# A written order for the first eight attention blocks, and moves of splits, sums and loads behind it

## The chip, the cores and the metric

The kernel runs on one core of a Trainium2 chip. A core has five engines with an instruction queue each: TensorE (PE in the views) for matrix products, VectorE (DVE), ScalarE (ACT), GpSimd (POOL) and SyncE (SP), which here only issues DMA transfers. The metric is the time of one execution in device microseconds, as a median of several runs; the profile is of one execution more, whose span is given beside it. TensorE's clock has two levels, 1.2 and 2.4 GHz; the granted clock in the views is the mean share of the upper one.

## The reference

Windowed attention, then a mixture of four experts, then a second feed-forward layer, all in float32 (w_in, w_out and alpha are drawn in float64):

```python
B, H, S, D = 2, 8, 576, 64                  # window 64
scores = q @ k.T / sqrt(D);  mask = (0 <= rel) & (rel < 64)
attn = exp(where(mask, scores, -1e9) - max);  attn /= sum + 1e-9
x = (attn @ v)                              # -> (1152, 512)
p = probs / (probs.sum(-1) + 1e-9)
y = sum(p[:, e] * (relu(x @ w1[e]) @ w2[e]) for e in range(4))    # w1 512 x 1024
h = y @ w_in                                # 512 x 2048
out = (max(h, 0) + alpha * min(h, 0)) @ w_out
```

## The kernel before, in words

Every product outside attention is done in three passes with operands split into a high part (rounded to fp32r) and a low part (the rest): high by low, low by high, high by high. ACT makes the high part, DVE or POOL the low part. So each operand tile, of weights or of tokens, costs one copy and one subtraction, and each result of a first product costs a copy (the activation) and a subtraction for its own halves, which the second product reads. In names, the last letter h or l is the part: w1h, w1l, xah, xal, hch, hcl.

**Stages.** The hidden width is cut into pieces of 512: stages 0 to 7 are the experts (two pieces each), stages 8 to 11 the second layer. A stage has first products and second products. In stages 1 to 11 the first products are seven per token half and column pair (a Strassen-like scheme over sums of weight blocks and of token blocks; units `A(s, p, i)`, banks X, Z and W in the views), and the second products are nine tiles of 128 tokens (units `B(s, p, t)`, tiles o). Stage 0 is done in four chunks of tokens without that scheme, since the tokens come out of attention at the same time: units `LC(c, f)` are the first products (tiles h0_c_f), units `BC(c, t)` the second ones (tiles oc). The list `order` holds all units in the order in which TensorE does them.

**Attention.** There are 18 blocks j of 64 queries. A block is a sequence of steps, and the list `steps` sets their order: `S` (scores, TensorE) with the mask and row minimum on DVE (sm, st), `E` (exponentials, four ACT instructions, p), `N` (divisors on two small DVE instructions, then p times them on POOL), `PT` (transposes on TensorE and the copy ptr on ACT or DVE), `PV` (product with v, and its splits into xah/xal or xch/xcl), `W` (a split of a stage-0 weight piece, `split_w1`), `Q` (a load of q), `X` (a token sum and split for the scheme, tiles tr and xt). Before the first unit the program emits steps up to the chunk's last PV and four steps more; behind each LC and BC unit it emits some more, until all are out at END.

**Behind the units.** After the unit's own instructions the loop runs what `plan` has put there: `w_sums` (four sums of weight blocks on POOL, tile sr), `w_split` (wfh, wfl), `split_w2` (w2h, w2l), and for stage 8 `x_sum` and `x_split` of the new tokens. From chunk 3 on, low parts are emitted one unit later than their high parts (`late["wait"]`, `settle`). Then come as many steps of a background job as `pace` gives: `conv_steps` turns the float64 pieces of w_in and w_out into float32 (32 pieces, tiles wd and ct; a step on ACT, one on DVE, one on DVE with the next load, one on DVE and POOL with a store to DRAM later). Last come the loads of weights, which are placed behind the last use of the tile whose buffer they take. In stages 8 to 11 the activation has more steps: `activate` runs a DVE step (heads) and then a copy on ACT and a subtraction on POOL (tails, hh and hl), of which some may be held back.

All queues are in program order. So what an engine does next is set by where these lists put it, and an instruction that waits holds what stands behind it on its engine.

## Time and profile before

| | before |
|---|---|
| median of 3 runs | 633.32 us (632.99 to 634.52) |
| profiled execution | 634.3 us |
| its span | 632.5 us |
| TensorE busy | 612.8 us (97%) |
| DVE, ACT, POOL busy | 462.6, 315.7, 285.4 us |
| mean granted clock | 0.992 |

The span is what the profile shows from the first to the last instruction; 1.8 us of the profiled execution lie outside of it. Busy times add an engine's instructions; a matmul's end is modelled, so a starved TensorE can look busy. TensorE's share of 97% means that at most 20 us of the span are without a matmul, 5.58 of them ahead of the first one.

### The profile page before, as it was taken

The page shows a single profiled execution, that of the slowest core. Times are in us where ns is not written, and L with a number is a line of the kernel's source. Part 1 is how long each engine was busy: PE and PEld are TensorE (multiplying, and loading weights), DVE is VectorE, ACT ScalarE, POOL GpSimd, SP SyncE. Part 2 cuts the span into 40 slices and gives each one's busy share as a digit, 9 for nine tenths or more (in the row PEclk, how much of TensorE's full clock was granted, in tenths as well). Part 3 has the DMA queues.
Part 4 walks back from the last instruction along what each step waited for, and adds up shares of the span by engine and source line. Part 5 has one row for each costly group of instructions (what it writes and reads, how often), then busy time and mean ns, then how long its engine had stood idle before and what let it go on. Part 6 is the DMA issues. An engine that isn't in the chain of part 4 may idle for free.

```text
span 632.5 us, 10897 instructions
## 1 busy us (share of the span) xinstructions
PE 612.8 (97%) x4032; PEld 548.9 (87%) x4032; DVE 462.6 (73%) x933; ACT 315.7 (50%) x789; POOL 285.4 (45%) x301
## 2 busy tenths in 40 slices
PE   4899999999999999999999999999999999999998
PEld 3688789989989988989989988989788978988986
DVE  3766649778789788788789788757867789763642
ACT  5756526633724624624724624636766662751730
POOL 5645651143443466053443463614735676661440
PEclk8899989999999999999999999999999999999999
DMA  9842001415316225324316224012302124110012
GB/s 323 310 153 68 2 1 64 138 33 183 118 46 205 84 84 183 100 68 167 118 54 196 84 83 150 18 35 98 135 1 108 59 103 136 34 63 1 2 50 101
DMA packets 31653, 62.60 MB, mean 99 GB/s; under 512 B 2288, under 2 KB 11760, under 8 KB 30576
## 3 DMA queue, kind: packets, MB, share of 16 engines
q1 hardware_dynamic: 31600, 61.90, 29.0%
q8 instruction: 32, 0.52, 0.3%
q14 instruction: 21, 0.17, 0.1%
HBM read 51.14 MB, written 10.75 MB: 98 GB/s over the span
## 4 chain that ended last, share of the span: by engine, by line
PE 83%; DVE 5%; ACT 4%; DMA 2%; POOL 2%; issue 2%; SPq 0%; ACTq 0%; POOLq 0%; DVEq 0%
PE o L545 40%; PE X L431 19%; PE Z L431 9%; PE W L431 4%; PE oc L533 4%; PE h L500 3%; ACT p L327 1%; DMA ws<-in_moe_w_dram 1%; PE pv L357 1%; DMA wd<-in_moe_w_in_dram 1%; POOL hl L526 1%; PE s L309 1%; DVE w2l L212 1%; PE pt L340 1%; ACT w2h L219 1%
## 5 line engine op out<-in xcount | busy, mean ns | idle before, releaser
L545 PE MATMUL o<-w2h,hl 128*128 128x512 f32 (+1 forms) x400 | 155.7, 389 | 0.6 <-POOL hl L526 0.5
L545 PE MATMUL o<-w2l,hh 128*128 128x512 f32 (+1 forms) x400 | 155.6, 389 | 0.4 <-ACT hh L525 0.4
L545 PE MATMUL o<-w2h,hh 128*128 128x512 f32 (+1 forms) x400 | 154.9, 387 | 0.0
L292 POOL TENSOR_TENSOR ct<-ct 128x512 f32<-128x512 f32 x32 | 42.7, 1335 | 133.3 <-DVE ct L291 58.1
L545 PEld LDWEIGHTS o<-w2h,hl 128*128 128x128 f32 x400 | 75.1, 188 | 18.3 <-POOL hl L526 3.2
L545 PEld LDWEIGHTS o<-w2l,hh 128*128 128x128 f32 x400 | 75.2, 188 | 15.0 <-ACT hh L525 0.6
L545 PEld LDWEIGHTS o<-w2h,hh 128*128 128x128 f32 x400 | 75.2, 188 | 14.9
L564 DVE SCALAR_TENSOR_TENSOR acc<-o,pn,acc 128x512 f32<-128x512 f32 x63 | 47.1, 748 | 40.7 <-PE o L545 40.6
L187 POOL TENSOR_TENSOR sr<-ws 128x256 f32<-128x256 f32 x44 | 41.6, 944 | 58.9 <-DVE wfl L212 53.0
L212 DVE SCALAR_TENSOR_TENSOR w2l<-ws,w2h 128x512 fp32r<-128x512 f32 x48 | 43.8, 918 | 25.6 <-ACT w2h L219 25.2
L431 PE MATMUL X<-xth,wfl 128*128 128x256 f32 (+1 forms) x264 | 57.4, 298 | 2.8 <-DVE z L442 1.7
L431 PE MATMUL X<-xtl,wfh 128*128 128x256 f32 (+1 forms) x264 | 56.6, 296 | 0.0
L431 PE MATMUL X<-xth,wfh 128*128 128x256 f32 (+1 forms) x264 | 56.6, 296 | 0.0
L293 POOL TENSOR_TENSOR ct<-ct 128x512 f32<-128x512 f32 x32 | 48.3, 1508 | 2.5
L280 ACT ACTIVATE ct<-wd 128x512 f32<-128x512 f32 x32 | 21.3, 665 | 50.8 <-DVE ct L286 50.8
L219 ACT ACTIVATE wfh<-sr 128x1024 fp32r<-128x1024 f32 x22 | 23.1, 1056 | 45.8 <-POOL sr L187 45.8
L431 PEld LDWEIGHTS X<-xth,wfl 128*128 128x128 f32 x264 | 42.5, 190 | 3.8 <-DVE z L442 2.3
L431 PEld LDWEIGHTS X<-xth,wfh 128*128 128x128 f32 x264 | 42.7, 190 | 0.0
L431 PEld LDWEIGHTS X<-xtl,wfh 128*128 128x128 f32 x264 | 42.6, 190 | 0.0
L568 DVE TENSOR_TENSOR acc<-o,acc 128x512 f32<-128x512 f32 (+1 forms) x28 | 18.7, 668 | 29.7 <-PE o L545 29.7
L526 POOL TENSOR_TENSOR hl<-s,hh 128x256 fp32r<-128x256 f32 (+1 forms) x16 | 13.4, 860 | 56.7 <-ACT hh L525 56.7
L438 ACT ACTIVATE s<-X 128x256 f32<-128x256 f32 (+1 forms) x44 | 18.0, 411 | 40.1 <-PE X L431 40.0
(157 smaller groups left out, 1440.5 us busy)
## 6 DMA issues: line engine op xcount, KB each, us to landing
ws<-in_moe_w_dram SPq DMA_DIRECT2D x16, 1024.0 KB, 5.9
wd<-in_moe_w_in_dram SPq DMA_DIRECT2D x16, 512.0 KB, 3.8
cv<-ct SPq DMA_DIRECT2D x32, 256.0 KB, 3.0
wd<-in_moe_w_out_dram SPq DMA_DIRECT2D x16, 512.0 KB, 3.7
ws<-cv SPq DMA_DIRECT2D x8, 1024.0 KB, 5.2
v<-in_v_dram SPq DMA_DIRECT2D x16, 256.0 KB, 5.4
q<-in_q_dram SPq DMA_DIRECT2D x6, 384.0 KB, 6.7
out_dram<-acc SPq DMA_DIRECT2D x8, 256.0 KB, 2.0
```

The source lines that it names most:

```text
L187: e.tensor_tensor(out=t4[:, o], in0=x, in1=y, op=op)
L212: nc.vector.scalar_tensor_tensor(out=lv, in0=src, scalar=1.0, in1=hv.bitcast(F32), op0=ALU.mult, op1=ALU.subtract)
L219: nc.scalar.activation(out=hv, in_=src, func=AF.Copy)
L280: nc.scalar.activation(out=a, in_=top.bitcast(F32), func=AF.Abs, scale=LIFT)
L292: nc.gpsimd.tensor_tensor(out=y, in0=y, in1=e, op=ALU.mult)
L293: nc.gpsimd.tensor_tensor(out=y, in0=r, in1=y, op=ALU.add)
L431: nc.tensor.matmul(ps, lhsT=w[:, d, :], rhs=x[:, d, :], start=(first and m == 0), stop=(m == 5), skip_group_check=True)
L500: nc.tensor.matmul(ps, lhsT=w[:, d * P:(d + 1) * P], rhs=x[:, d, :], start=(m == 0), stop=(m == 3 * KD - 1))
L526: nc.gpsimd.tensor_tensor(out=hl, in0=g, in1=hh.bitcast(F32), op=ALU.subtract)
L533: nc.tensor.matmul(ps, lhsT=h_c[c, f][a][:, t * P:(t + 1) * P], rhs=w_t[2, 0, f][b], start=(n == 0), stop=(n == 3 * NF - 1))
L545: nc.tensor.matmul(ps, lhsT=h_t[s, p, f][a][:, t * P:(t + 1) * P], rhs=w_t[2, s, f][b][:, cols], start=(n == 0), stop=(n == 3 * NF - 1))
L564: nc.vector.scalar_tensor_tensor(out=at, in0=ps, scalar=sc, in1=at, op0=ALU.mult, op1=ALU.add)
```

## The change

The first 8 blocks' steps are written out by hand, with four blocks' exponentials one behind the other; the mask on DVE becomes a step `M` of its own. The splits of stage-0 weight pieces 2 and 3 move behind the first two LC units, the second ones' w2 splits by one unit; the even pieces' low parts go to DVE and the odd ones' to POOL, where it was the other way round. From block 8 on a loop goes on as before, with the X steps one block earlier and the last block's N ahead of a PT. Loads of w1 pieces from stage 2 on are placed no earlier than behind the fourth product of the stage before; some sums and splits of weights, the token sums of stage 8 and the steps of the conversion move to other units.

```diff
--- before.py
+++ after.py
@@ -226,7 +226,7 @@
         hv, lv = [x.rearrange("p (k m) -> p k m", k=KD) for x in w_tiles(1, 0, f)]
         src = ws_t[1, 0][:, :, f * P:(f + 1) * P]
         nc.scalar.activation(out=hv, in_=src, func=AF.Copy)
-        e = nc.vector if f % 2 else nc.gpsimd
+        e = nc.gpsimd if f % 2 else nc.vector
         e.tensor_tensor(out=lv, in0=src, in1=hv.bitcast(F32), op=ALU.subtract)
 
     def split_w2(s, f):
@@ -294,7 +294,7 @@
             done.append((conv[which, s][:, f, :], ct[:, 4 + n % 3]))
         store()
 
-    v_t, ws_t, wd_t, w_t, wf_t, h_t, p_t, pt_t = {}, {}, {}, {}, {}, {}, {}, {}
+    v_t, ws_t, wd_t, w_t, wf_t, h_t, m_t, p_t, pt_t = {}, {}, {}, {}, {}, {}, {}, {}, {}
 
     def att_S(j):
         g, jb = divmod(j, GB)
@@ -313,6 +313,10 @@
                     start=True, stop=True, skip_group_check=True,
                 )
 
+        m_t[j] = sv, m
+
+    def att_M(j):
+        sv, m = m_t.pop(j)
         sm = ab.tile([P, NP, P], F32, tag="sm", bufs=2, name=f"sm{j}")
         st = ab.tile([P, 4, NP], F32, tag="st", bufs=4, name=f"st{j}")
         pt = ab.tile([P, NP, P], F32, tag="p", bufs=4, name=f"p{j}")
@@ -340,7 +344,7 @@
             nc.tensor.transpose(ps[:, hp * P:(hp + 1) * P], pt[:, hp, :], ident)
         t = ab.tile([P, NP, P], F32, tag="ptr", bufs=2, name=f"ptr{j}")
         src = ps.rearrange("p (a k) -> p a k", a=NP)
-        if j % 2 and j >= NF:
+        if j in (0, 1) or j % 2 and j >= NF:
             nc.vector.tensor_copy(out=t, in_=src)
         else:
             nc.scalar.activation(out=t, in_=src, func=AF.Copy)
@@ -361,7 +365,7 @@
         c = max(c for c in range(NCH) if CHUNK[c] <= j * BLK)
         o = j * BLK - CHUNK[c]
         hi, lo = [x[:, :, o:o + BLK] for x in xc[c]]
-        if (j + 1) * BLK in CHUNK:
+        if j == 2 or (j + 1) * BLK in CHUNK:
             nc.scalar.activation(out=hi, in_=pv, func=AF.Copy)
             nc.vector.tensor_tensor(out=lo, in0=pv, in1=hi.bitcast(F32), op=ALU.subtract)
             nc.vector.tensor_copy(out=src, in_=pv)
@@ -458,7 +462,7 @@
             evict(s, p, 2 * u + 1, 0, ps, True)
             del sets[s, p, u]
         if s >= S1:
-            activate(1 if i > 2 else 0, int(i < 5) if s == S1 else (2, 0, 4)[min(i, 2)])
+            activate(1 if i > 2 else 0, 0 if s == S1 else (2, 0, 4)[min(i, 2)])
         else:
             low_parts(1)
 
@@ -601,37 +605,35 @@
         nc.sync.dma_start(out=alph, in_=alpha)
 
         NG = NBLK // GB
-        steps = []
-        for j in range(NBLK + 4):
+        steps = [(op, int(j)) for op, j in (x.split("_") for x in (
+            "S_0 M_0 E_0 S_1 M_1 E_1 N_0 S_2 M_2 E_2 N_1 S_3 M_3 E_3 Q_3 PT_0 N_2 PT_1 N_3 PV_0 W_0 PT_2 PV_1 W_1 "
+            "S_4 M_4 PT_3 PV_2 PV_3 S_5 E_4 M_5 N_4 E_5 S_6 M_6 N_5 Q_4 E_6 PT_4 S_7 M_7 N_6").split())]
+        for j in range(8, NBLK + 4):
             last = (j - 3) * BLK in CHUNK[1:]
-            pv = [("PV", j - 4)] if 0 <= j - 4 < NBLK else []
-
+            pv = [("PV", j - 4)] if j - 4 < NBLK else []
+            apart = j - 1 < 14
             if last:
                 steps += pv
-            apart = 6 <= j - 1 < 14
             if apart:
                 steps.append(("E", j - 1))
-            if 0 <= j - 3 < NBLK:
+            if j == NBLK:
+                steps.append(("N", j - 1))
+            if j - 3 < NBLK:
                 steps.append(("PT", j - 3))
-            if 3 < j <= NBLK and not apart:
+            if not apart and j < NBLK:
                 steps.append(("N", j - 1))
             if j < NBLK:
-                steps.append(("S", j))
-                if not 6 <= j < 14:
+                steps += [("S", j), ("M", j)]
+                if j >= 14:
                     steps.append(("E", j))
-            if 0 < j <= 3:
-                steps.append(("N", j - 1))
             if not last:
                 steps += pv
             if apart:
                 steps.append(("N", j - 1))
-            if 2 <= j < 2 + NF:
-                steps.append(("W", j - 2))
-            if j % GB == 0 and 3 <= j // GB + 2 < NG:
+            if j % GB == 0 and j // GB + 2 < NG:
                 steps.append(("Q", j // GB + 2))
-
-            if 13 <= j < 18:
-                steps.append(("X", j - 13))
+            if 12 <= j < 17:
+                steps.append(("X", j - 12))
         pos = [0]
 
         def att_step():
@@ -643,6 +645,8 @@
                     load_k(1, 0, S)
             elif op == "S":
                 att_S(j)
+            elif op == "M":
+                att_M(j)
             elif op == "E":
                 att_E(j)
             elif op == "N":
@@ -695,8 +699,10 @@
         def plan(unit, fn, tid, *args):
             work.setdefault(at[unit], []).append((fn, tid, args))
 
+        for f in range(2, NF):
+            plan(("LC", 0, f - 2), split_w1, None, f)
         for f in range(NF):
-            plan(("LC", 0, f), split_w2, (2, 0), 0, f)
+            plan(("LC", 0, min(f + 1, 3)), split_w2, (2, 0), 0, f)
         for s in range(1, NST):
             if s == 1:
                 lc, b = [[(k, NCH - 1, t) for t in range(3)] for k in ("LC", "BC")]
@@ -709,13 +715,15 @@
                 b = [("B", s - 1, x, t) for x in range(2) for t in range(NTT[x])]
                 if s == S1 + 1:
                     b = [("B", S1, 1, t) for t in (3, 3, 4, 4, 0, 1)]
-                plan(("A", s - 1, 1, 0 if s > S1 else 2), w_sums, (1, s), s, 0, nc.gpsimd)
-                plan(b[2], w_sums, (1, s), s, 1, nc.gpsimd)
-                for n, part in ((0, A11), (0, A22), (1, SA1)):
+                late_sums = s > S1 + 1
+                behind = 2 * (s > S1 + 1)
+                plan(b[1] if behind else ("A", s - 1, 1, 0 if s > S1 else 2), w_sums, (1, s), s, 0, nc.gpsimd)
+                for n, part in ((0, A11), (0, A22), (1 + behind, SA1)):
                     plan(b[n], w_split, (1, s), s, 0, part)
-                for n, part in ((2, A11), (3, A22), (4, SA1)):
+                plan(b[2 + behind], w_sums, (1, s), s, 1, nc.gpsimd)
+                for n, part in ((2, A11), (3, A22), (4 + behind, SA1)):
                     plan(b[n], w_split, (1, s), s, 1, part)
-            units = [(0, 1), (0, 2), (1, 0), (1, 1)]
+            units = [(0, 0), (0, 1), (1, 0), (1, 1)]
             if s in (1, S1):
                 units = [(int(s == 1), i) for i in (0, 0, 1, 1)]
             for f, (p, i) in enumerate(units):
@@ -729,9 +737,11 @@
                    (("B", S1 - 1, 1, 2), 0, (3, 5), (), first), (("B", S1 - 1, 1, 3), 0, (3, 5), (), second),
                    (("B", S1 - 1, 1, 4), 0, (4,), (), first), (("B", S1 - 1, 1, 4), 0, (4,), (), second)]
         for o in half[1]:
-            changes += [(("A", S1, 0, 2), 1, (), (1,), o), (("A", S1, 0, 3), 1, (), (2,), o),
-                        (("B", S1, 0, 2), 1, (0, 1), (), o), (("B", S1, 0, 3), 1, (2,), (3,), o),
-                        (("B", S1, 0, 0), 1, (3, 5), (4,), o), (("B", S1, 0, 1), 1, (4,), (), o)]
+            changes += [(("B", S1, 0, 2), 1, (0,), (1,), o), (("B", S1, 0, 3), 1, (1,), (), o),
+                        (("B", S1, 0, 0), 1, (2, 5), (3,), o), (("B", S1, 0, 1), 1, (3,), (), o),
+                        (("A", S1, 1, 0), 1, (4,), (), o)]
+        for unit, f in ((("B", S1, 0, 2), 2), (("B", S1, 0, 1), 4)):
+            changes += [(unit, 1, (), (f,), o) for o in half[1]]
         for unit, p, splits, sums, (o, w) in changes:
             for f in splits:
                 if f == 0:
@@ -764,24 +774,27 @@
                     uses.setdefault(tid, []).append(n)
         tids = sorted(uses, key=lambda x: uses[x][0])
         tids = [(1, 0)] + tids
-        uses[1, 0] = [-1]
+        uses[1, 0] = [at["LC", 0, 1]]
         loads = {}
         for n, tid in enumerate(tids):
             if n >= 2:
-                loads.setdefault(uses[tids[n - 2]][-1] + (tids[n - 2][1] > 0), []).append(tid)
+                free = uses[tids[n - 2]][-1] + (tids[n - 2][1] > 0)
+                if tid[0] == 1 and tid[1] > 1:
+                    free = max(free, at["A", tid[1] - 1, 0, 3])
+                loads.setdefault(free, []).append(tid)
 
         marks = [steps.index(("PV", CHUNK[c + 1] // BLK - 1)) + 1 for c in range(NCH)]
         per = [len(LC(c) + BC(c)) for c in range(NCH)]
-        while pos[0] < marks[0] + 4:
+        while pos[0] < marks[0] + 2:
             att_step()
         for tid in loads.get(-1, ()):
             load_w(tid)
         def pace(op, s=0, p=0, i=0):
             if op == "A":
-                return int(2 <= s < S1 and i < 2 + (s == S1 - 1) or S1 < s < NST - 1 and i in (1, 2))
-            if op != "B" or s in (S1 - 1, NST - 2, NST - 1) or (s, p) == (S1, 0):
+                return int(2 <= s < S1 and i < 2 or S1 < s < NST - 1 and i < 2)
+            if op != "B" or s in (S1 - 1, NST - 2, NST - 1) or (s, p) == (S1, 0) or s > S1 and (p, i) == (0, 0):
                 return 0
-            return 1
+            return 1 + (s == 1 and p == 0 and i % 2)
 
         pend = []
         for i, unit in enumerate(order):
@@ -813,7 +826,7 @@
                 l2_unit(*unit[1:])
                 if unit[1] == S1 - 1:
                     pend.append((i + 2, unit[2], unit[3]))
-            if i == 0:
+            if i == 2:
                 p_prep()
             while pend and pend[0][0] <= i:
                 x2_unit(*pend.pop(0)[1:])
```

How this moves instructions on three engines. ACT, from the first weight copy on (block 3's exponentials are p3; w1h_0_f are the copies of stage 0's weight pieces). Before:

```order
L327 ACTIVATE p2_219,st2_218<-sm2_217,st2_218 128x128 x4
L228 ACTIVATE w1h_0_0_231<-ws1_0_147 128x512
L346 ACTIVATE ptr0_240<-pt0_235 128x512
L327 ACTIVATE p3_254,st3_253<-sm3_252,st3_253 128x128 x4
L228 ACTIVATE w1h_0_1_266<-ws1_0_147 128x512
L346 ACTIVATE ptr1_277<-pt1_272 128x512
L327 ACTIVATE p4_294,st4_293<-sm4_292,st4_293 128x128 x4
L228 ACTIVATE w1h_0_2_317<-ws1_0_147 128x512
L346 ACTIVATE ptr2_326<-pt2_321 128x512
L327 ACTIVATE p5_343,st5_342<-sm5_341,st5_342 128x128 x4
L228 ACTIVATE w1h_0_3_366<-ws1_0_147 128x512
L346 ACTIVATE ptr3_375<-pt3_370 128x512
```

After:

```order
L331 ACTIVATE p2_219,st2_218<-sm2_217,st2_218 128x128 x4
L331 ACTIVATE p3_243,st3_242<-sm3_241,st3_242 128x128 x4
L228 ACTIVATE w1h_0_0_288<-ws1_0_147 128x512
L350 ACTIVATE ptr2_297<-pt2_292 128x512
L228 ACTIVATE w1h_0_1_313<-ws1_0_147 128x512
L350 ACTIVATE ptr3_339<-pt3_334 128x512
L369 ACTIVATE xah0_81<-pv2_341 128x4x64
L369 ACTIVATE xah0_81<-pv3_355 128x4x64
L331 ACTIVATE p4_329,st4_328<-sm4_327,st4_328 128x128 x4
L515 ACTIVATE hch0_0_397<-h0_0_0_384 128x256
L228 ACTIVATE w1h_0_2_401<-ws1_0_147 128x512
L331 ACTIVATE p5_407,st5_406<-sm5_405,st5_406 128x128 x4
```

p3 and the weight copies changed places, ptr0 and ptr1 left ACT, the second part of xah came to it, and the copies of weight pieces 2 and 3 stand behind the first two products' copies hch.

DVE at the end of attention, from the last mask of block 17 on (TENSOR_SCALAR and RECIPROCAL are the divisors of block 17; ptr15 and ptr17 are copies that PV15 and PV17 read). Before:

```order
L320 ISA sm17_1160,st17_1161<-s17_1_1151,mask_73 128x128
L320 ISA st17_1161 128x1
L512 SCALAR_TENSOR_TENSOR hcl2_3_1185<-h0_2_3_1171,hch2_3_1184 128x256
L369 COPY xr1_86<-pv13_1188 128x4x64
L389 TENSOR_TENSOR tr0_4_0_1200<-xr0_85,tr0_2_0_1055 128x512
L344 COPY ptr15_1209<-pt15_1204 128x512
L332 TENSOR_SCALAR st17_1161<-st17_1161 128x4
L333 RECIPROCAL st17_1161<-st17_1161 128x4
L369 COPY xr1_86<-pv14_1214 128x4x64
L539 TENSOR_SCALAR acc1_80<-oc2_0_1226,pn_77 128x512
```

After:

```order
L324 ISA sm17_1181,st17_1182<-s17_1_1155,mask_73 128x128
L324 ISA st17_1182 128x1
L373 COPY xr1_86<-pv13_1192 128x4x64
L336 TENSOR_SCALAR st17_1182<-st17_1182 128x4
L337 RECIPROCAL st17_1182<-st17_1182 128x4
L348 COPY ptr15_1212<-pt15_1207 128x512
L543 TENSOR_SCALAR acc1_80<-oc2_0_1214,pn_77 128x512
L373 COPY xr1_86<-pv14_1228 128x4x64
L373 COPY xr1_86<-pv15_1247 128x4x64
```

The divisors of block 17 stand ahead of ptr15 now, the token sum tr0_4 is gone from this place (it stands ahead of them, before the masks).

POOL at the start of stage 8 (tr1 are token sums of the second half, hl8 low parts that stage 8's second products read). Before:

```order
L389 TENSOR_TENSOR tr1_1_0_4991<-raw1_4701 128x320
L389 TENSOR_TENSOR tr1_1_160_4993<-raw1_4701 128x320
L389 TENSOR_TENSOR tr1_2_0_5022<-raw1_4701,tr1_1_0_4991 128x320
L389 TENSOR_TENSOR tr1_2_160_5024<-raw1_4701,tr1_1_160_4993 128x320
L526 TENSOR_TENSOR hl8_0_0_5006<-s18_0_0_4914,hh8_0_0_5005 128x256
L526 TENSOR_TENSOR hl8_0_2_5018<-s18_0_1_4923,hh8_0_2_5017 128x256
L526 TENSOR_TENSOR hl8_0_1_5034<-z18_0_0_4948,hh8_0_1_5033 128x256
L526 TENSOR_TENSOR hl8_0_3_5048<-z18_0_1_4957,hh8_0_3_5047 128x256
L526 TENSOR_TENSOR hl8_0_0_5006<-u28_0_0_4979,hh8_0_0_5005 128x256
```

After:

```order
L530 TENSOR_TENSOR hl8_0_0_5000<-s18_0_0_4914,hh8_0_0_4999 128x256
L530 TENSOR_TENSOR hl8_0_2_5012<-s18_0_1_4923,hh8_0_2_5011 128x256
L530 TENSOR_TENSOR hl8_0_1_5028<-z18_0_0_4946,hh8_0_1_5027 128x256
L530 TENSOR_TENSOR hl8_0_3_5042<-z18_0_1_4955,hh8_0_3_5041 128x256
L530 TENSOR_TENSOR hl8_0_0_5000<-u28_0_0_4977,hh8_0_0_4999 128x256
L530 TENSOR_TENSOR hl8_0_2_5012<-u28_0_1_4985,hh8_0_2_5011 128x256
L530 TENSOR_TENSOR hl8_0_1_5028<-r8_0_1_0_5078,hh8_0_1_5027 128x256
```

The four token sums left POOL for DVE; what stood behind them comes first.

## Rows read from the trace of the kernel before

**Rows 1.** Stretches: length, each engine's busy time, granted clock, DMA share, GB/s.
```profile
0.00:25.40 25.40, 14.29 (x213) 10.87 (x213) 12.37 (x76) 16.95 (x67) 15.85 (x31) 0.87 0.96 345
25.40:35.02 9.62, 9.62 (x124) 8.67 (x121) 8.31 (x40) 6.90 (x26) 3.56 (x6) 1.00 0.44 146
62.00:79.50 17.50, 15.72 (x191) 13.30 (x189) 11.48 (x47) 9.48 (x34) 11.30 (x13) 1.00 0.00 1
79.50:85.50 6.00, 5.99 (x48) 5.06 (x49) 1.87 (x4) 0.38 (x1) 5.68 (x10) 0.72 0.01 3
149.20:196.10 46.90, 46.90 (x278) 42.67 (x277) 38.02 (x64) 22.56 (x48) 18.10 (x16) 1.00 0.37 128
243.00:290.60 47.60, 47.31 (x278) 42.79 (x277) 39.16 (x65) 21.24 (x46) 19.59 (x17) 1.00 0.36 117
384.40:436.10 51.70, 50.58 (x307) 45.52 (x306) 36.77 (x64) 24.88 (x56) 21.24 (x22) 1.00 0.15 54
436.10:486.60 50.50, 49.49 (x287) 42.97 (x285) 36.87 (x65) 36.15 (x83) 26.66 (x29) 1.00 0.21 73
486.60:535.50 48.90, 47.53 (x279) 42.78 (x278) 42.73 (x62) 26.86 (x63) 33.95 (x34) 1.00 0.33 114
```

**Rows 2.** Chain that ended last, in the start: start us, us, what.
```profile
12.35 0.63 ACT w1h L228
12.98 0.48 ACT ptr L346
13.47 1.54 ACT p L327 x8
...
25.47 3.07 PE h L500 x24
28.54 0.44 PE pt L340 x4
28.98 0.59 PE s L309 x16
...
35.09 1.12 PE oc L533 x4
```

**Rows 3.** Waits of TensorE behind 62 us: total, times, longest.
```profile
PE pt L340 <- POOL p L334: 1.8, 1, 1.8
PE X L431 <- DVE z L442: 1.7, 3, 1.0
PE X L431 <- ACT u L438: 1.1, 1, 1.1
```

**Rows 4.** Timeline of DVE: start, us, tiles, then [idle before <- what ended it].
```profile
15.56 0.69 DVE L230 TENSOR_TENSOR w1l<-ws,w1h 128x512 fp32r<-128x512 f32 x1 [2.53 <-ACT w1h L228]
```

**Rows 5.** Timeline of POOL in the start.
```profile
16.68 1.04 POOL L334 TENSOR_TENSOR p<-p,st 128x512 f32<-128x512 f32 x1 [1.35 <-DVE st L333]
```

**Rows 6.** Timeline of TensorE before the end of attention.
```profile
69.57 0.67 PE L309 MATMUL s<-kt,q 64*64 64x128 f32 x16
...
71.22 0.64 PE L500 MATMUL h<-xch,w1h 128*128 128x256 f32 x4
```

**Rows 7.** Chain that ended last, in the middle of stage 7.
```profile
420.14 2.76 PE o L545 x12
```

**Rows 8.** Timeline of DVE in stage 4.
```profile
250.35 1.22 DVE L212 SCALAR_TENSOR_TENSOR w2l<-ws,w2h 128x512 fp32r<-128x512 f32 x1
```

**Rows 9.** Timeline of POOL in stage 4.
```profile
250.99 1.18 POOL L187 TENSOR_TENSOR sr<-ws 128x256 f32<-128x256 f32 x1
```

**Rows 10.** Tile ws in stages 1 to 4: min/median/max ns, first and last start.
```profile
L212 DVE SCALAR_TENSOR_TENSOR w2l<-ws,w2h x13: 676/693/1823, 115.3 to 247.0; 128x512 fp32r<-128x512 f32 x13
...
DMA to landing us min/median/max: 5.1/5.7/7.0
```

**Rows 11.** Timeline of ACT in stage 7.
```profile
389.77 0.67 ACT L279 ACTIVATE ct<-wd 128x512 f32<-128x512 uint32 x1 [1.45 <-DMA wd<-in_moe_w_in_dram]
```

**Rows 12.** Timeline of POOL in stage 8.
```profile
441.64 2.60 POOL L389 TENSOR_TENSOR tr<-raw,tr 128x320 f32<-128x320 f32 x2
```

## The prediction

> **What bounds the kernel now.** I read the busy times by stretch first, then the list of what TensorE waits for, then the start and the few late waits one by one. In the first view a steady stage (149.2 to 196.1) shows TensorE busy for 46.90 us of 46.90 [rows 1]: there nothing that the other four engines do can save time unless it shortens TensorE's own program, and the change leaves every product as it is. What can be won is TensorE's idle time, and it lies in six places. The first 25.40 us hold only 14.29 us of TensorE work; the stretch 62.00 to 79.50 lacks 1.78 us, and the one behind it runs at a granted clock of 0.72; stage 4 (243.0 to 290.6) is 0.70 us longer than a steady one; stage 7 lasts 51.70, stage 8 50.50, stage 9 48.90 [rows 1]. Stage 7 has seven extra transposes and stage 8 two, of about 0.44 us each (the four-matmul transpose at 28.54 [rows 2]). So what these stages are above a steady one, work aside, is 51.70 − 46.90 − 3.08 = 1.72, 50.50 − 46.90 − 0.88 = 2.72, and 48.90 − 46.90 = 2.00. Some of that is counted as busy, since a starved matmul's end is modelled; the length of the stage is the better measure. The list of waits names the causes behind 62 us: 1.8 us for a normalised block from POOL, 1.7 for running sums on DVE, 1.1 for a copy on ACT [rows 3].
>
> **Part 1, the start.** The program orders that count are TensorE's, ACT's and DVE's up to the first second product oc. In both kernels TensorE has done the same by then: ten score blocks, seven transposes, six PV blocks, four h products. So the gain is the difference in the start of oc, 35.09 now [rows 2], and not that in the start of h.
>
> Before, block 3's exponentials stand behind the first weight copy and a ptr copy on ACT and take 1.54 us from 13.47 [rows 2]; its divisors stand on DVE behind a w1l subtraction that waits 2.53 us for the second weight copy [rows 4]; so POOL multiplies p3 only at 16.68, for 1.04 [rows 5]. After, E3 follows E2 at once. The two ACT pieces ahead of it, the weight copy at 12.35 and the ptr copy at 12.98, go behind: 1.1 us [rows 2]; E3 ends near 13.9, its divisors follow two ptr copies on DVE (about 0.7 each, as the w1l of the same 128x512, 0.69 [rows 4]; the first is done while E3 runs), and p3 is ready at about 15.4 in place of 17.7. Then PT3 0.4 to 0.9 and PV3 0.6 to 1.2 (at full and at half clock; an eight-head PV is put at the price of a score block, 0.59), ptr3 0.5 [rows 2], xah and xal 0.4 each, half the elements of that w1l: 3.6 with the hand-overs at the upper end, so h starts near 19.05 in place of 25.47.
>
> From there the in-order queues take most of it back. On DVE, hcl of the first product (it waits for h, 1.5 us as half of 3.07 [rows 2], and its copy on ACT) and w1l of piece 2 stand ahead of block 5's masks and block 4's divisors. I follow it: h ends 20.6, hch 20.9, hcl 21.3, w1h 21.4, w1l 22.1, M5 23.0, divisors 23.3, p4 on POOL 24.4, PT4 24.8 at TensorE, which finished h1 at 22.7: a wait of 2.1 us. The same loop again, with E5 ahead of hch1 on ACT and w2h ahead of w2l on DVE, gives PT5 at 28.75 with a wait of 1.25, and PT6 at 32.5 with 0.5. TensorE's work from h to oc is 9.62 us before [rows 1], and two S blocks of 0.59 and one transpose of 0.44 more now [rows 2]: 11.24. Sum: 19.05 + 11.24 + 3.85 = 34.1, and oc at 34.1 to 34.4: −0.7 to −1.0. I take −0.5, as a chain of some 15 hand-overs done by hand is rather too short than too long. Bounds: with no wait behind h, oc at 30.3, −4.8; with a granted clock as low as in the first 25.40 us (0.87 [rows 1]) over the 11.24 us, which is 1.5 us, and 0.5 of hand-overs, +1.5. The DVE row with its 2.53 us of idle is the evidence that one waiting instruction holds what stands behind it: block 3's divisors were computable earlier. The Trainium skill ("PSUM — Partial Sum Buffer", section Engine vs sequencer instructions) says that the queues of ScalarE, VectorE and GpSimd are strict first-in first-out; by it the early h buys only what the queues behind it can keep up with, and the row agrees.
>
> Splitting the masks from the scores, and giving the even w1l pieces to DVE, cost nothing by themselves: the same instructions on the same tiles. p_prep two units later has no user before the first oc is evicted.
>
> **Part 2, the end of attention.** TensorE waits 1.8 us for p17 before PT17 [rows 3], and the 6.00 us behind it have a granted clock of 0.72 [rows 1]. Before, block 17's divisors stand on DVE behind hcl of h2.3, the copy of PV13, the sum tr4 and ptr15, and on POOL p17 stands behind an xtl. After, the X steps come a block earlier, so xtl is out of the way, and the divisors stand ahead of ptr15. By the same walk, with the times of before up to h2.3 (S17 at 69.57, the last h piece at 71.22 [rows 6]): masks behind hcl of h2.3 at 72.6, E17 to 74.3, divisors 74.7, p17 75.7. TensorE comes to PT17 behind h2.3 (71.8), PV13, PT15, oc2.0 (2.76, the price of an o of as many matmuls [rows 7]), PV14, PT16 and PV15, with 0.59 and 0.44 as above: 77.4. So the wait goes with 1.7 us to spare: −1.78. The low clock follows the only idle time of that stretch, and I let it go with it: 6.00 × (1 − 0.72) = −1.68. Against it the copy of ptr17 on DVE before PV17, partly uncovered, +0.4. Sum −3.05. Bounds 0 (p17 still late) and −3.5.
>
> **Part 3, the late stages.**
> - Stage 4: a sum on DVE is late because a w2l before it took 1.22 us at 250.35 [rows 8], beside sums on POOL [rows 9], where the fastest w2l took 0.68 and the slowest 1.82 [rows 10]. The load of the next w1 piece is now asked for behind the fourth product, some 6.3 us into the stage (worked out under the slower rival), and takes 5.7 [rows 10]: POOL's sums can't start before 255, and the w2 splits come one product earlier, so they part. −0.70. The Trainium skill ("SBUF — State Buffer", section Who interferes with whom) states that a DVE instruction with two SBUF inputs contends with a GpSimd instruction that reads SBUF; by it every pair that the change brings together would cost up to half a microsecond, and the rows agree in direction.
> - Against the change: the conversion steps are shifted against the weight splits in every stage, so DVE and POOL pieces that were apart may now meet; one new stall of stage 4's size, +0.70.
> - Stage 7: ACT's conversion copy at 389.77 waits 1.45 us for its DMA [rows 11], and the u copy of the products stands behind it: 1.1 us at TensorE [rows 3]. All ACT conversion steps now lie ahead of stage 7. Of 1.72 I take −1.4; bounds 0 and −1.72.
> - Stage 8: POOL's sums of the second feed-forward input take 2.60 us for two at 441.64 [rows 12], ahead of the hl parts, which TensorE's second products read. All eight sums go to DVE behind the first product tiles, and the tails are no longer held back. DVE is busy 36.87 of 50.50 us there [rows 1], which has room for four more sums at even the 1.3 us that POOL takes for one. Of 2.72 I take −2.0; bounds 0 and −2.72.
> - Stage 9: sums on POOL and w2l on DVE at the same time made a running sum on DVE late, the largest of the three such waits (1.0 [rows 3]); for the stages behind 9 the sums move among the second products. Of 2.00 I take −1.7; bounds 0 and −2.00.
>
> **The sum.** −0.5 − 3.05 − 0.7 + 0.7 − 1.4 − 2.0 − 1.7 = −8.65. The profiled execution took 634.3 (a span of 632.5 and 1.8 around it), 1.0 above the median of 633.32; 625.65 on its scale, 624.7 on that of the median.
>
> **The rivals.**
> - The start is kept in full: no wait behind h, −4.8 in place of −0.5. For it: POOL and ACT are far from busy. Against it: the DVE chain from h to p4 above is 3.8 us long and TensorE has 2.1 us of work for it. 633.3 − 8.65 − 4.3 = 620.4.
> - The late waits only move: the conversion has the same instructions, and DVE is busy 42.73 of 48.90 us in stage 9 [rows 1]. Then parts 1 and 2 alone stay, −3.55: 629.8.
> - The same, and the start at its bound: +1.5 − 3.05 = −1.55: 631.8, no change that can be told. (The smallest difference that the runs can tell from none is about 0.3%, 1.9 us.)
> - Slower: the delayed loads come too late. In each of the stages 1 to 10 the next stage's w1 piece (1 MB) is now asked for only behind the fourth product. Nine second products of 2.76 us [rows 7] leave 22.1 of the 46.90 us for fourteen products, 1.58 each; asked for at +6.3, landing 5.7 us later (7.0 at most [rows 10]), it is there at +12 to +13.3. Its first split comes with the first second product, at +22.1, so 9 us are to spare. If stores of converted weights, which wait on SyncE's queue for POOL, hold the request for longer than that, every next stage starts late by the rest. To end above 635.2 the ten stages must lose 10.6 us, 1.06 each: the request would be some 10 us late in every one. At 2 us each it ends at 644.7.
>
> **How the numbers follow.** Forecast 0.60, start in full 0.10, late waits only moved 0.18, no change 0.06, slower 0.06. So faster 0.88, same 0.06, slower 0.06. The likeliest, 624.7, has a range of its own of 622.5 to 627.0: the start by 1 us either way, and of the 5.8 us from stages 4 and 7 to 9 at least 4.0 and at most 7.1. The range for the time goes from 620.5, which takes in half of the rival with the full start, to 630.5, past the one with moved waits; 0.17 are left out.
>
> **What would show it.** Right: h near 19, PT4, PT5 and PT6 with waits for POOL's p in the list, oc between 33.5 and 35; no wait at PT17 and a granted clock of 1.00 behind it; stage 4, 8 and 9 at 47, 48.5 and 47.2, stage 7 at 50.3. Wrong: oc near 30 or behind 36, a new line in the list of waits above 1 us in a steady stage, or products that wait for a load.

## The result, and the profile after

The changed kernel takes 626.55 us in the median (625.8 to 627.91) against 633.58 (632.99 to 634.52): a ratio of 0.989, interval 0.9867 to 0.9914, or 7.0 us less. The forecast was 8.65 less, 624.7. Run again beside other kernels on another chip, it took 625.95 against 634.5, a ratio of 0.9867 (0.9853 to 0.9881): 8.55 less. The page of the first profile, part 1:

```profile
span 625.1 us, 10881 instructions
PE 610.3 (98%) x4032; PEld 548.1 (88%) x4032; DVE 471.1 (75%) x940; ACT 316.2 (51%) x788; POOL 281.5 (45%) x295
```

The same view by stretches as [rows 1] (length, busy time of PE, PEld, DVE, ACT, POOL, granted clock, DMA share, GB/s), with the stages at their new places:

```profile
0.00:25.40 25.40, 16.83 (x216) 13.46 (x216) 13.03 (x70) 14.08 (x55) 12.20 (x28) 1.00 0.93 330
...
62.00:79.50 17.50, 17.50 (x200) 14.70 (x199) 12.76 (x48) 10.02 (x37) 12.90 (x15) 1.00 0.05 18
79.50:84.33 4.83, 4.66 (x48) 3.76 (x49) 2.23 (x5) 0.42 (x2) 4.59 (x8) 1.00 0.01 3
...
241.70:288.60 46.90, 46.90 (x278) 42.66 (x277) 39.76 (x64) 21.44 (x47) 20.59 (x17) 1.00 0.36 116
382.40:432.50 50.10, 50.10 (x306) 45.29 (x304) 35.26 (x61) 24.05 (x55) 19.44 (x20) 1.00 0.15 53
432.50:481.00 48.50, 48.50 (x288) 43.33 (x286) 39.35 (x69) 36.81 (x83) 23.33 (x25) 1.00 0.22 75
481.00:527.90 46.90, 46.90 (x278) 42.66 (x277) 40.69 (x60) 26.82 (x63) 32.88 (x32) 1.00 0.29 99
```

Stages 4, 7, 8 and 9 are as long as TensorE's own work. The granted clock of the first row is to be read with care: this trace holds no clock record before 18.34, which the view counts as 1.00, and the matmuls there take the time of the lower level (a four-matmul transpose 1.11 us at 11.30 where it takes 0.66 at 26.43, both below). The waits of TensorE in the whole execution (total, times, longest) are down to the start and 0.2 us at the end of attention; of [rows 3] nothing is left:

```profile
PE s L309 <- DMA kt<-in_k_dram: 6.3, 1, 6.3
PE pt L344 <- POOL p L338: 4.0, 4, 1.8
PE s L309 <- DMA q<-in_q_dram: 1.1, 1, 1.1
PE pv L361 <- DVE ptr L348: 0.2, 1, 0.2
```

The timeline of TensorE at the start, in the same profile (start, us, tiles, then the idle time before and what ended it):

```profile
6.28 2.84 PE L309 MATMUL s<-kt,q 64*64 64x128 f32 x48 [6.28 <-DMA kt<-in_k_dram]
...
11.30 1.11 PE L344 MATMUL pt<-ident,p 128*128 128x128 f32 x4
...
20.74 0.71 PE L504 MATMUL h<-xah,w1l 128*128 128x256 f32 x4
...
26.43 0.66 PE L344 MATMUL pt<-ident,p 128*128 128x128 f32 x4 [1.81 <-POOL p L338]
...
30.95 0.66 PE L344 MATMUL pt<-ident,p 128*128 128x128 f32 x4 [1.63 <-POOL p L338]
...
34.73 0.66 PE L344 MATMUL pt<-ident,p 128*128 128x128 f32 x4 [0.29 <-POOL p L338]
...
36.53 0.50 PE L537 MATMUL oc<-w2l,hch 128*128 128x512 f32 x1
```

The first product h starts 4.7 us earlier than before (20.74 for 25.47 [rows 2]), and the first oc 1.4 us later. In between lie three waits for a block's p, 3.73 us in all. The timeline of DVE shows what p4 stood behind:

```profile
22.85 0.42 DVE L516 SCALAR_TENSOR_TENSOR hcl<-h,hch 128x256 fp32r<-128x256 f32 x1 [1.47 <-ACT hch L515]
23.37 0.69 DVE L230 TENSOR_TENSOR w1l<-ws,w1h 128x512 fp32r<-128x512 f32 x1
...
24.82 0.17 DVE L336 TENSOR_SCALAR st<-st 128x4 f32<-128x4 f32 x1
25.02 0.18 DVE L337 RECIPROCAL st<-st 128x4 f32<-128x4 f32 x1
```

DVE idles 1.47 us for hch of the first product, then does w1l and block 5's masks, and only then block 4's divisors, whose inputs were ready at 22.1, when E4 had ended on ACT. POOL's product, which PT4 at 26.43 waits for, follows the divisors:

```profile
25.34 1.04 POOL L338 TENSOR_TENSOR p<-p,st 128x512 f32<-128x512 f32 x1 [4.59 <-DVE st L337]
```

At the end of attention, PT17 now follows without a wait, and PV17 waits 0.17 us for ptr17:

```profile
79.39 0.66 PE L344 MATMUL pt<-ident,p 128*128 128x128 f32 x4
...
80.83 0.69 PE L361 MATMUL pv<-ptr,v 128*64 128x64 f32 x16 [0.17 <-DVE ptr L348]
```

So that runs can be compared, each is cut by TensorE's timeline at four places: the first score block (which waits for a transfer, at 5.4 to 6.3 us, not a matter of the change), the first oc, the first product of stage 1, and the last matmul. Before: 29.44, 67.08 and 527.34 us between them. After: 30.25, 64.34 and 521.11. That is +0.81, −2.74 and −6.23, with +0.70 for the first transfer: −7.46 of a span that went from 632.5 to 625.1.

### The profile page after: what moved, and what is told of

It is laid out like the page before. It is cut to its first block, busy times and chain, and to the rows that moved or that the text cites. A ratio compares the mean times of both kernels' runs of the same rounds, so it can differ in the third digit from the quotient of the medians.

```text
span 625.1 us, 10881 instructions
## 1 busy us (share of the span) xinstructions
PE 610.3 (98%) x4032; PEld 548.1 (88%) x4032; DVE 471.1 (75%) x940; ACT 316.2 (51%) x788; POOL 281.5 (45%) x295
## 4 chain that ended last, share of the span: by engine, by line
PE 95%; ACT 2%; DMA 1%; DVE 1%; issue 0%; POOL 0%; SPq 0%; POOLq 0%
PE o L549 43%; PE X L435 23%; PE Z L435 11%; PE W L435 6%; PE oc L537 4%; PE h L504 4%; PE pv L361 2%; PE pt L344 1%; PE s L309 1%; ACT p L331 1%; DMA kt<-in_k_dram 1%; PE x L582 1%; POOL p L338 0%; ACT ptr L350 0%; ACT w1h L228 0%
## 5 line engine op out<-in xcount | busy, mean ns | idle before, releaser
L435 PE MATMUL Z<-xth,wfl 128*128 128x320 f32 (+1 forms) x176 | 37.9, 296 | 0.0
```

Of the source, the lines that this page charges most:

```text
L435: nc.tensor.matmul(ps, lhsT=w[:, d, :], rhs=x[:, d, :], start=(first and m == 0), stop=(m == 5), skip_group_check=True)
```

## The experiments

All edits are to the changed kernel unless said otherwise.

| run | median, us | ratio to before (interval) | first scores to first oc | oc to stage 1 |
|---|---|---|---|---|
| changed, again (e1) | 625.95 | 0.9867 (0.9853 to 0.9881) | 29.27 | 64.35 |
| old order of the first blocks (e2) | 627.3 | 0.9888 (0.9874 to 0.9902) | 31.95 | 63.86 |
| late parts alone (e3) | 628.04 | 0.9907 (0.989 to 0.9925) | 29.58 | 67.33 |
| block 4's divisors ahead (e4) | 625.39 | 0.9861 (0.9844 to 0.9878) | 28.80 | 64.31 |
| blocks 4 and 5 ahead (e9) | 624.95 | 0.9836 (0.9819 to 0.9853) | 28.16 | 64.33 |
| matmuls ahead of the data (e10) | 626.5 | 0.9863 (0.9843 to 0.9883) | 28.86 | 64.30 |
| both (e11) | 625.78 | 0.9851 (0.9832 to 0.987) | 27.75 | 64.32 |
| blocks 4, 5 and 6 ahead (e12) | 624.92 | 0.9843 (0.9816 to 0.9871) | 27.49 | 65.34 |

**The changed kernel once more (e1).** 

> The changed kernel once more, on the chip of the next three. Theory (the start is what was mis-sized; it loses 0.7 to 1.4 us where a gain of 0.5 was forecast): first oc again 0.7 us or more later than in the kernel before, counted from the first score block (before: 35.02 - 5.58 = 29.44; after: 36.53 - 6.28 = 30.25), ratio 0.987 to 0.991. Rival (the late first transfer of the one profile made the loss): first oc at 29 us or less behind the first score block.

The theory falls, and the rival with it: oc comes 29.27 us behind the first scores, 0.17 sooner than before and 0.98 sooner than in the first profile, with the same instructions. The difference is the clock. By stretches of this run (the first stretch again lies ahead of the trace's first clock record, at 8.69, and its three score blocks take 2.84 us, the time of the lower level):

```profile
5.77:8.69 2.92, 2.84 (x48) 2.44 (x48) 1.64 (x15) 1.30 (x7) 0.00 (x0) 1.00 1.06 380
8.69:12.10 3.41, 1.32 (x20) 0.87 (x20) 2.77 (x23) 3.41 (x19) 2.01 (x2) 1.00 1.04 387
12.10:15.52 3.42, 3.29 (x26) 2.52 (x28) 2.59 (x8) 2.11 (x11) 2.13 (x4) 0.50 1.04 386
15.52:25.76 10.24, 8.35 (x136) 6.88 (x140) 6.09 (x27) 7.83 (x26) 5.78 (x9) 1.00 0.96 343
25.76:29.17 3.41, 3.41 (x28) 2.98 (x20) 3.31 (x19) 1.80 (x10) 1.65 (x2) 0.50 0.37 101
```

Here the clock is at its upper level from 8.69 to 12.10 and again from 15.52 to 25.76, in the first profile from 18.34 on, so h starts 13.47 us behind the first scores in place of 14.46. The second low stretch costs nothing: it falls on the third h product, behind which TensorE waited 1.63 us for p5 in the first profile, and that wait is gone here.

The four profiles e5 to e8, further down, change only what lies behind the start: up to the first oc they run the same instructions. So there are six profiles of one start:

| us | first profile | e1 | e5 | e6 | e7 | e8 |
|---|---|---|---|---|---|---|
| first scores to first h | 14.46 | 13.47 | 12.99 | 12.95 | 13.03 | 13.19 |
| first h to first oc | 15.79 | 15.80 | 15.80 | 15.80 | 16.77 | 16.79 |
| sum | 30.25 | 29.27 | 28.79 | 28.75 | 29.80 | 29.98 |

The sum differs by 1.5 us from profile to profile, with 29.44 and 29.58 for the old order (before, e3) in the midst of it. So one profile can't tell a gain or loss of the start that is under 1.5 us by the sum; the time from h to oc is the steadier measure.

**The order of the first eight blocks alone (e2).** 

> The changed kernel with the first eight blocks' steps, the stage-0 splits, p_prep and the load of the second w1 piece in the order of before; the end of attention and the late stages as changed. Theory: the new start loses, so this is faster than the changed kernel by 0.7 to 1.4 us: 625.2 to 625.9 in the median where that has 626.6. Rival (the new start gains and the profile was an unlucky one): slower than the changed kernel by 0.5 us or more, 627.1 or above.

```diff
-        steps = [(op, int(j)) ... "S_0 M_0 E_0 S_1 ... S_7 M_7 N_6")]
+        for j in range(8):    # the loop of before, with M behind S
...
-        while pos[0] < marks[0] + 2:
+        while pos[0] < marks[0] + 4:
```

1.35 us slower than the changed kernel on the same chip, so by the numbers the rival holds. But the run is no clean undoing: emission behind a unit goes by a count of steps, M counts as one now, and so a transposition more (PT7) stands ahead of the first oc, where TensorE waits 1.24 us for its p. What the new start is worth by itself e2 does not tell.

**The late parts alone, in the kernel before (e3).** 

> The kernel before with the changes behind attention alone (loads, sums, token sums of stage 8, held tails, pace of the conversion); attention as before in all its blocks. Theory (the parts add up, the late ones give 6.2): 627.4 in the median, stages 4, 7, 8, 9 of 46.9, 50.1, 48.5, 46.9 us, and the wait of 1.8 for p17 still there. Rival (part of the late gain needs the earlier attention): 628.5 or more, one of these stages over 0.7 us longer.

The kernel before, with these taken from the change and nothing else:

```diff
-            activate(1 if i > 2 else 0, int(i < 5) if s == S1 else (2, 0, 4)[min(i, 2)])
+            activate(1 if i > 2 else 0, 0 if s == S1 else (2, 0, 4)[min(i, 2)])
...
+                if tid[0] == 1 and tid[1] > 1:
+                    free = max(free, at["A", tid[1] - 1, 0, 3])
...
```

(the new units of w_sums, w_split, split_w2, x_sum and x_split and the new pace among them).

6.46 us less than before on the same chip, with stages of 46.90, 50.13, 48.54 and 46.90 us and the wait of 1.8 for p17 where it was: the theory holds, the late parts need nothing from the earlier ones. Against e1 the whole of stage 0 is worth 2.1 us: 0.31 up to the first oc, 2.98 from there to stage 1, less 0.28 for the first transfer, by the profiles, 3.0 in all; the 0.9 between that and the medians I leave to the scatter (e3's runs go from 627.18 to 630.55). The 0.31 is less than the same start's spread of 1.5, so no gain of the start is shown; the 2.98 are the end of attention.

**Block 4's divisors ahead of the first hcl (e4).** 

> The changed kernel with two steps more emitted ahead of the first h product, so that block 5's masks and block 4's divisors stand on DVE ahead of the product's hcl and of the third w1l. Theory (the in-order DVE queue makes TensorE wait 1.8 us for p4): that wait goes, p4 is ready near 22.5 to 23, before the second h product ends at 24.5; the wait for p5 (1.6) stays or grows by part of it; 0.8 to 1.8 us faster than the changed kernel, 624.8 to 625.8. Rival (E4 or the POOL queue holds p4, the order on DVE doesn't matter): the wait stays over 1.2 us and the time within 0.5 us of the changed kernel.

```diff
-        while pos[0] < marks[0] + 2:
+        while pos[0] < marks[0] + 4:
```

The wait for p4 is gone, and the next one took up most of it (timeline of TensorE):

```profile
23.13 0.60 PE L344 MATMUL pt<-ident,p 128*128 128x128 f32 x4
...
28.55 0.87 PE L344 MATMUL pt<-ident,p 128*128 128x128 f32 x4 [2.60 <-POOL p L338]
```

So the order on DVE was the cause of the first wait, as forecast. The gain of 0.56 in the medians is under the 0.8 expected, and within the scatter of both; from h to oc it is 15.69 us for 15.80, with a low granted clock from 28.84 to 32.26 in it. A gain in time is not shown.

**Blocks 4 and 5 ahead (e9).** 

> The changed kernel with the divisors of blocks 4 and 5 ahead of the first h product's hcl on DVE (six steps emitted ahead of that product in place of two, and block 5's divisors moved ahead of block 6's scores). Theory (the waits for p4 and p5 come from DVE's and ACT's order alone): no wait of over 0.5 us for p4 or p5, one for p6 of up to 1 us (its divisors still stand behind the third hcl and a w2l), first oc 25.5 to 27.5 us behind the first score block where the changed kernel has 29.3 to 30.3; 2 to 3.5 us faster than the changed kernel, ratio to before 0.981 to 0.984. Rival (the work moved ahead makes ACT late with hch and w1h, so that the third h product waits instead): first oc within 1 us of the changed kernel's, ratio 0.985 or more.

```diff
-            "... S_5 E_4 M_5 N_4 E_5 S_6 M_6 N_5 Q_4 E_6 PT_4 S_7 M_7 N_6")
+            "... S_5 E_4 M_5 N_4 E_5 N_5 S_6 M_6 Q_4 E_6 PT_4 S_7 M_7 N_6")
...
-        while pos[0] < marks[0] + 2:
+        while pos[0] < marks[0] + 6:
```

Neither p4 nor p5 is waited for. In their place the list of waits of TensorE has, behind the fourth score block:

```profile
PE pt L344 <- POOL p L338: 2.2, 2, 1.4
...
PE pv L361 <- ACT ptr L350: 1.0, 1, 1.0
PE h L504 <- DVE w1l L230: 0.3, 1, 0.3
```

(0.9 of the first line is p1's, and 1.36 p6's.) From h to the first oc, 1.1 us are kept: 14.68 us in e9 and 14.67 in e11 (below), in place of 15.79 to 16.79 in the six profiles of the changed start. The medians, from two chips, differ by 1.0 (624.95 and 625.95, with the kernel before at 634.72 and 634.5 beside them), and all runs of e9 lie below all of e1. That is between the two: less than the theory's 2 to 3.5, though the ratio, 0.9836, is in its range; the waits for p4 and p5 went as it said, that for p6 is longer than the 1 us it allowed, and the wait for w1l, of the tiles that the rival had late, is 0.3.

**Block 6 as well (e12).** 

> The kernel with the divisors of blocks 4 and 5 ahead, and now block 6's scores, masks and exponentials between the first two h products, its divisors behind the second hcl and one w2l, and the copy of ptr4 ahead of E7. Theory (each wait left at the start is one in-order queue's; 1.36 for p6 and 1.0 for ptr4 go when their makers stand earlier): both waits under 0.4 us, first oc 25.3 to 26.8 us behind the first score block where the run with two blocks' divisors ahead has 28.2, ratio to before 0.979 to 0.982. Rival (ACT is the bound from here on: with E5, E6 and the copies of four products and weights in one row it hands hch, w1h or w2h late, and TensorE waits for these): first oc at 27.5 or more, ratio 0.982 to 0.985.

```diff
-            "... S_5 E_4 M_5 N_4 E_5 S_6 M_6 N_5 Q_4 E_6 PT_4 S_7 M_7 N_6")
+            "... S_5 E_4 M_5 N_4 E_5 N_5 S_6 M_6 E_6 PT_4 N_6 S_7 M_7 Q_4")
...
-        while pos[0] < marks[0] + 2:
+        while pos[0] < marks[0] + 6:
...
+                if unit in (("LC", 0, 0), ("LC", 0, 1)):
+                    goal = marks[0] + (9, 14)[unit[2]]
...
```

p6 is in time (0.9 of what is left is p1's), but new waits come up for copies on ACT and DVE, and the first oc's own operands are late for the first time:

```profile
PE pv L361 <- DVE ptr L348: 1.1, 2, 0.9
PE pt L344 <- POOL p L338: 1.0, 2, 0.9
PE pv L361 <- ACT ptr L350: 0.9, 1, 0.9
...
PE oc L537 <- DVE w2l L212: 0.2, 1, 0.2
```

The first oc comes at 27.49, 0.67 us sooner than in e9, and 1.0 us more is spent from there to stage 1 (65.34 for 64.33), 0.8 of it in the first tile oc: the time is that of e9. The rival holds by the ratio, 0.9843; 27.49 is on its edge. Between h and oc ACT is now busy for 11.45 and DVE for 10.57 of 14.00 us (by stretches). That an order can only move the wait from one tile to the next there I conclude from these shares; no run shows it.

**Matmuls ahead of the first data (e10), and both (e11).** 

> The changed kernel with 14 matmuls of 128 columns on a zeroed tile at the start, while TensorE waits for its first data; their result is not used. Theory (the low granted clock from the first score block on, up to 18.3 us in one profile, costs about 1 us and makes the runs scatter): granted clock 1.00 from the first scores, first oc 0.5 to 1.5 us earlier than in the changed kernel, ratio to before 0.984 to 0.986. Rival (the chain of ACT and POOL sets the start, whatever the clock, or the clock falls again in the first idle time): ratio 0.986 to 0.988, no difference.

> Both of the last two edits. Theory (they add up, since the one takes waits away and the other shortens work between them): ratio 0.978 to 0.982, the fastest of all. Rival (either the warm clock is lost in the waits before the fourth block or the work at half clock was hidden): like the run with the divisors alone.

```diff
+        zero, warm = acc[0][:, 0, 0:P], psum("warm")[:, 0:P]
+        nc.vector.memset(zero, 0.0)
+        for n in range(14):
+            nc.tensor.matmul(warm, lhsT=zero, rhs=zero, start=True, stop=True, skip_group_check=True)
```

```profile
1.05 5.94 PE L591 MATMUL warm<-acc 128*128 128x128 f32 x28 [1.05 <-DVE acc L589]
6.92 1.54 PE L309 MATMUL s<-kt,q 64*64 64x128 f32 x48
10.19 0.67 PE L309 MATMUL s<-kt,q 64*64 64x128 f32 x16 [1.74 <-DMA q<-in_q_dram]
11.39 0.66 PE L344 MATMUL pt<-ident,p 128*128 128x128 f32 x4 [0.53 <-POOL p L338]
12.92 0.85 PE L344 MATMUL pt<-ident,p 128*128 128x128 f32 x4 [0.88 <-POOL p L338]
13.70 1.12 PE L361 MATMUL pv<-ptr,v 128*64 128x64 f32 x16
```

The timeline of e10 shows the clock up for the first scores (1.54 us for three blocks in place of 2.84), but they start later, behind 5.94 us of extra matmuls; then TensorE waits for q, p0 and p1, and the clock falls again, at 13.25 (in e1 at 12.10). No gain in either run: 28.86 us to the first oc lies among the six profiles without the matmuls, 626.5 is 0.6 above e1, and e11 is 0.8 above e9. The rivals hold. A shorter row of matmuls, one that ends ahead of the first data, wasn't run.

**Four of the late parts undone, one at a time.** One profile each. Lengths of stages from first product to first product, where they differ by over 0.1 us:

| | stage 2 | 4 | 5 | 7 | 8 | 9 | 10 |
|---|---|---|---|---|---|---|---|
| before | 46.91 | 47.59 | 46.90 | 51.59 | 50.60 | 48.86 | 46.90 |
| changed | 46.90 | 46.90 | 46.90 | 50.13 | 48.49 | 46.90 | 46.89 |
| loads as before (e5) | 47.63 | 46.90 | 47.41 | 50.13 | 48.54 | 46.90 | 46.89 |
| pace as before (e6) | 46.90 | 46.90 | 46.90 | 51.03 | 48.50 | 46.91 | 47.30 |
| stage 8's sums, tails as before (e7) | 46.90 | 46.90 | 46.90 | 50.13 | 50.63 | 46.90 | 46.90 |
| weight sums, w2 splits as before (e8) | 47.48 | 46.90 | 46.90 | 50.12 | 48.48 | 47.78 | 47.60 |

> The changed kernel, with the loads of the w1 pieces where they stood before (behind the last use of their buffer alone). Theory (the later load keeps POOL's sums of weights away from DVE's w2l): a stage between 1 and 6 is again about 0.7 us longer than 46.9, with a wait of TensorE for z on DVE beside a w2l of over 1.1 us. Rival (it was the shift of the conversion steps or the earlier w2 splits that parted them): stages 1 to 6 stay at 46.9 to 47.0, and the span moves by less than 0.3 apart from the start.

```diff
-                if tid[0] == 1 and tid[1] > 1:
-                    free = max(free, at["A", tid[1] - 1, 0, 3])
```

Two stages are longer, but by another way than the theory's: no wait for z, two for u on ACT (0.47 and 0.26). In stage 2, by rows from the timelines of SyncE, ACT and TensorE:

```profile
143.84 0.39 SPq L144 DMA_DIRECT2D ws<-in_moe_w_dram  x1
145.45 0.34 SPq L155 DMA_DIRECT2D wd<-in_moe_w_out_dram  x1
```

```profile
150.82 0.68 ACT L279 ACTIVATE ct<-wd 128x512 f32<-128x512 uint32 x1 [0.78 <-DMA wd<-in_moe_w_out_dram]
```

```profile
152.39 0.50 PE L435 MATMUL X<-xth,wfl 128*128 128x256 f32 x2 [0.47 <-ACT u L442]
```

The 1 MB of weights, asked for early, stands ahead of a piece of the conversion; that lands 5.3 us after its issue, ACT waits for it, and u stands behind. It is the stall of stage 7 before [rows 11]. So, with the other parts in place, the delayed loads are worth 1.24 us, by clearing the way for the conversion and not by moving POOL's sums.

> The changed kernel, with the conversion steps spread as before. Theory (ACT's conversion copy that waits for its DMA in stage 7 held the copy u): stage 7 (from its first product to that of stage 8) 51.6 us again where the changed kernel has 50.1, with a wait for ACT. Rival (another part, the earlier w2 splits, made that gain): stage 7 at 50.1 to 50.4.

```diff
-                return int(2 <= s < S1 and i < 2 or S1 < s < NST - 1 and i < 2)
+                return int(2 <= s < S1 and i < 2 + (s == S1 - 1) or S1 < s < NST - 1 and i in (1, 2))
...
-            return 1 + (s == 1 and p == 0 and i % 2)
+            return 1
```

Stage 7 loses 0.90 of its 1.46, not all, and with a wait for z on DVE, not for ACT: without the early load ahead of it the conversion's transfer is in time, and what is left are the conversion's own DVE steps there (1.18 and 1.40 us), beside its POOL steps; another step of the second's kind, at 383.08, took 0.43. The running sums stand behind them (DVE, then TensorE):

```profile
387.30 1.40 DVE L283 TENSOR_SCALAR ct<-ct 128x512 uint32<-128x512 uint32 x1
```

```profile
390.33 0.51 PE L435 MATMUL X<-xth,wfl 128*128 128x256 f32 x2 [0.64 <-DVE z L446]
```

Stage 10 loses 0.4.

> The changed kernel, with stage 8's token sums split between POOL and DVE and its tails held back as before. Theory (they make the 2.1 us of stage 8): stage 8 50.6 us again where the changed kernel has 48.5. Rival (the earlier w2 splits or the weight sums of stage 9 do): within 0.5 us of 48.5.

```diff
-            activate(1 if i > 2 else 0, 0 if s == S1 else (2, 0, 4)[min(i, 2)])
+            activate(1 if i > 2 else 0, int(i < 5) if s == S1 else (2, 0, 4)[min(i, 2)])
...
-            changes += [(("B", S1, 0, 2), 1, (0,), (1,), o), (("B", S1, 0, 3), 1, (1,), (), o),
+            changes += [(("A", S1, 0, 2), 1, (), (1,), o), (("A", S1, 0, 3), 1, (), (2,), o),
...
```

All of it: 50.63. The theory holds for the sums and the tails together; the run doesn't part them.

> The changed kernel, with the weight sums and splits of the stages from 2 on and the four w2 splits of a stage at the units of before. Theory (weight sums on POOL beside w2l on DVE delay a running sum in stage 9): stage 9 48.9 us again where the changed kernel has 46.9. Rival (the conversion's pace does it): stage 9 at 47.2 or less.

```diff
-                plan(b[1] if behind else ("A", s - 1, 1, 0 if s > S1 else 2), w_sums, (1, s), s, 0, nc.gpsimd)
+                plan(("A", s - 1, 1, 0 if s > S1 else 2), w_sums, (1, s), s, 0, nc.gpsimd)
...
-            units = [(0, 0), (0, 1), (1, 0), (1, 1)]
+            units = [(0, 1), (0, 2), (1, 0), (1, 1)]
```

Stage 9 loses 0.88, not 1.96, stage 10 0.70 and stage 2 0.58. In stage 2 (DVE, then POOL):

```profile
154.37 1.78 DVE L212 SCALAR_TENSOR_TENSOR w2l<-ws,w2h 128x512 fp32r<-128x512 f32 x1
156.08 0.41 DVE L446 TENSOR_TENSOR z<-X,z 128x256 f32<-128x256 f32 x1
```

```profile
152.40 1.64 POOL L292 TENSOR_TENSOR ct<-ct 128x512 f32<-128x512 f32 x1 [1.74 <-ACT ct L279]
154.11 1.49 POOL L293 TENSOR_TENSOR ct<-ct 128x512 f32<-128x512 f32 x1
```

It is the stall of stage 4 before ([rows 8]), two stages earlier, with the conversion's POOL steps in the place of the weight sums: a w2l that takes 0.68 us alone takes 1.78 beside them, and z stands behind it. Undone singly the four parts cost 6.9 us, together 6.2; each shifts the others.

## Why the prediction was right, by its own steps

Its main line held: TensorE's own work is the bound in a steady stage, the gain is idle time, and the time came out inside the range, also inside the narrower one of 622.5 to 627.0, 1.9 us above the forecast in the first runs and 1.3 in e1 by medians (8.55 of 8.65 us there, against the kernel before on the same chip).

- **The start.** "−0.5" was mis-sized. Measured are +0.81 in the first profile, −0.17 in e1 and −0.69 to +0.54 in e5 to e8; the first transfer added +0.70 and +0.19 in the first two, which I had left out as it is not the change's. The waits were right: 1.81, 1.63 and 0.29 us for p4, p5 and p6 in the first profile against 2.1, 1.25 and 0.5 forecast, 3.73 in sum for 3.85. The term that failed is TensorE's work from h to oc: 11.24 by the sum, 12.06 in the first profile (15.79 less 3.73, at a granted clock of 1.00). A product h that stands alone there takes 1.70 us (22.92 to 24.62), half of two in a row 1.5 [rows 2]; a transposition takes 0.58 for the 0.44 that was counted. The path to h was wrong too, though its number was not: "near 19.05" is 13.47 us behind the first scores, and the six profiles have 12.95 to 14.46. I had counted PT3 and PV3 alone, behind p3. In the first profile p3 was ready at 16.05, and TensorE worked from PT1 at 12.73 up to h at 20.74 without a gap, at the lower level up to 18.34. So that h lay near the forecast is luck. e4, e9 and e12 show that DVE's order holds p4, that each wait that is taken away uncovers one behind it, and that 1.1 us is to be had of the 3.7.
- **The end of attention.** −3.05 forecast, −2.74 measured, with neither wait nor low clock left. That the clock would go with the wait is borne out: both profiles with the wait for p17 (before, e3) have a granted clock of 0.50 for 3.41 us behind it, from 80.05 and from 80.68, and none of the other twelve has. PV17 waits 0.17 for the copy of ptr17, within the 0.4 allowed. The last 0.3 I have not pursued.
- **Stage 4** gained its 0.69, but the reason given, that w2l and POOL's work part, is not what the runs show. POOL's sums did start later, at 255.87, but a w2l now meets POOL's conversion, 3 us into the stage in place of 7.5, and no wait of TensorE follows (DVE, then POOL):

```profile
244.63 1.78 DVE L212 SCALAR_TENSOR_TENSOR w2l<-ws,w2h 128x512 fp32r<-128x512 f32 x1
```

```profile
244.50 1.36 POOL L293 TENSOR_TENSOR ct<-ct 128x512 f32<-128x512 f32 x1
```

Stage 4 stays at 46.90 with the load as before (e5), and also in e6, e7 and e8: no part undone alone brings the 0.69 back, so which of them made it is open. For stage 2, e8 shows that the w2 splits' place relative to POOL's work counts, and that POOL's conversion steps do as the sums do. The rule of the Trainium skill quoted in the prediction ("SBUF — State Buffer", section Who interferes with whom) covers both: the row of e8 agrees with it, at 1.1 us for the pair. That is twice the half microsecond that the prediction allowed for a pair.
- **The new stall, +0.70,** didn't come: stages 1 to 6 are all at 46.9 to 47.0.
- **Stage 7** −1.46 for −1.4, of which the pace as before gives back 0.90 (e6). The other 0.56 I put down to the delayed loads, which clear the way for the transfer; e5 alone leaves stage 7 as it is, and no run undoes both. **Stage 8** −2.11 for −2.0, and e7 shows that it is the sums and the tails together. **Stage 9** −1.96 for −1.7, of which e8 gives back 0.88; what made the rest is open.
- **The delayed loads** were not late: no wait for one stands in the list, and the piece asked for at 247.45 in stage 4 was there 6.3 us later, for POOL's sums at 255.87, before the first second product at 264.05.

So the late stages gave 6.2 where 5.1 was forecast, mostly for the +0.70 that didn't come, the end of attention gave 0.3 less, and the start came out between 0.2 better and 1.3 worse than forecast. That the sum lies so near is in part luck: these errors have opposite signs.
